# Fewer unread products in the begin, and tile loads split into two transfers

## The chip, the cores and the metric

The kernel runs on one core of one Trainium2 chip. Its time is the device time of that core in microseconds (us). The engines of a core are TensorE (PE in the profile, with its weight loads as PEld), VectorE (DVE), ScalarE (ACT), GpSimd (POOL) and SyncE (SP, which in this kernel issues all transfers between HBM and the on-chip memory SBUF). Matrix products are written to PSUM, which is read by DVE and ACT. Each engine works through its own list of instructions in order, and an instruction waits on semaphores for what it needs.

## The reference

Three stages follow each other. Attention is in chunks: 4 batches, 8 heads, 768 positions, 64 values a head. Each chunk of 32 queries sees 8 memory keys, up to 16 keys to its left, its own 32 and up to 8 to its right:

```
scores = (q_c @ k_full.T) / sqrt(64)
a = exp(scores - max(scores));  a = a / (sum(a) + 1e-9)
out[c] = a @ v_full
```

The result is a matrix of 3072 tokens by 512. Two layers follow, each with a matrix of 512 x 2048 and one of 2048 x 512, held as 64-bit floats:

```
h = x @ w1_in;  x = (h * clip(h + 3, 0, 6) / 6) @ w1_out
h = x @ w2_in;  out = max(0.01 * h, h) @ w2_out
```

## The kernel before, in words

**Tiling.** The tokens are in six blocks of 512. A weight tile `f` (16 for each of the four matrices) is 128 x 512. A weight or an activation is split into a high part, rounded to the fast 32-bit format of PE, and the low part that is left; a product is then three products (high by high, low by high, high by low), each 128x512 on PE. `hidden` (products on L998) makes one tile of `h` for one block, `output` (L1047) adds its share to four banks of the result. Later parts (`seven`, `second`; L1322 and L1490) work on pairs of blocks with seven products in the place of eight.

**Weights.** `decode` (from L386) loads a tile of 64-bit floats as pairs of 32-bit words, 4096 bytes a partition, by one transfer (`load`, L393), and builds 32-bit floats from the bits: `scaled` (L396) on ACT, then `bits` (L400), `sign` (L404) and `low` (L408) on DVE. `split_w` makes high (a cast, L341) and low (a difference, L344).

**Attention.** `unit(j, quad)` is one attention unit: four heads, 384 positions. `half_unit(j, quad, gp)` is half of one. The begin has `unit(0, 0)`, `unit(0, 1)`, `half_unit(1, 0, 0)`, `half_unit(1, 1, 0)`, then the two other half units; their results are the first blocks. A unit loads queries and keys (`load_qk`: L491, two groups of chunks in one transfer, 448 KB; in a half unit L769, two pairs of heads in one transfer) and values (`load_v`, `load_whole`); copies keys into windows (`windows`, on DVE, ACT or POOL); makes scores (L544; L811 in a half unit), the softmax on DVE and ACT (L561 to L598; L825 to L862), transposes (L602; L866), copies them out of PSUM (`take_p`), and multiplies with the values (L622; L882). `to_x` casts the result to `xh` (ACT, L341) and takes the rest as `xl` (DVE, L344).

**Unread products.** `warm(n, after, home)` (L461) puts products of the identity with itself on PE: with no `home` in a bank of their own, `n` of 512 columns; with a `home` `n` of 256 columns, in the upper half of the second bank of that buffer. Their result is read by nobody. The last argument's buffer is `ac`, in which `half_unit(1, 1, 0)` has its scores. Each product is recorded as two. A group is tied to a mark: `s` scores, `t` transposes, `v` values of a unit or half unit, and its key (its rank) is just behind the mark's. Four groups come first, and five more in a loop at L1565.

**The order.** `schedule` is a planner that runs while the program is built. It simulates the engines, with a cost for each task, takes on each engine the ready task with the smallest key, and writes the instructions in that order. Transfers are counted by their issues and bytes, with eight in flight on SP (`LANES`); a task may be said to have several issues (`issues`). It also counts PE's instructions: 447 held at the start, 256 more at each fetch (`HELD`, `FETCHED`, `FETCH`). All tasks are ranked by `key`; loads of the begin have their keys in `LOADS` and `WEIGHTS`. A change of a cost, of issues or of a task can therefore move other instructions as well.

Of the kernel before, what the change touches and what calls it, by code (L numbers as in the profile page):

```python
# [9 lines left out]
F32 = mybir.dt.float32  # L10
F32R = mybir.dt.float32r
U32 = mybir.dt.uint32
# [5 lines left out]
B, H, S, D, NMEM = 4, 8, 768, 64, 8  # L18
# [5 lines left out]
QK = 2 * G + 2 * KW  # L24
# [32 lines left out]
RATE_QK, RATE, RATE_V, COLD = 380.0, 220.0, 300.0, 1.1  # L57
# [198 lines left out]
def tile_attn_moe_moe2(ctx: ExitStack, tc: tile.TileContext, raw, w1i, w1o, w2i, w2o, out):  # L256
    nc = tc.nc
# [24 lines left out]
    def make(b, kind=None):  # L282
        if b.tag in ("hx", "y") and b.tag not in pools:

            (attention if b.tag == "hx" else begin).close()
            pools[b.tag] = (ctx.enter_context(tc.tile_pool(name=b.tag, bufs=places[b.tag], space=PSUM, side="right" if b.tag == "hx" else "left")), [128, 512], F32)
        pool, shape, dt = pools[b.tag]
        if kind is not None:
            shape, dt = kind
        b.t = pool.tile(shape, dt, tag=b.tag, name=b.tag)  # L290
        return b.t
# [35 lines left out]
    def dma(nbytes, rate=250.0):  # L327
        return nbytes / rate
# [3 lines left out]
    def add(fn, opts, key, **kw):  # L332
        t = Task(fn, opts, key, **kw)
        tasks.append(t)
        return t
# [52 lines left out]
    def decode(src, f, key, early=None, after=(), place="wm", gate=(), late=0, own=True, split=None):  # L388

        t, m = Buf("w"), Buf(place)  # L390

        def load(e):
            nc.sync.dma_start(out=make(t, ([128, 512, 2], U32)).rearrange("p w s -> p (w s)"), in_=src[f])  # L393

        def scaled(e):
            nc.scalar.mul(make(m, ([128, 512], F32)), t.t[:, :, 1].bitcast(F32), SCALED)  # L396

        def bits(e):
            mu = m.t.bitcast(U32)
            nc.vector.tensor_scalar(out=mu, in0=mu, scalar1=3, scalar2=0x7FFFFFF8, op0=ALU.logical_shift_left, op1=ALU.bitwise_and)  # L400

        def sign(e):
            mu = m.t.bitcast(U32)
            nc.vector.scalar_tensor_tensor(out=mu, in0=t.t[:, :, 1], scalar=0x80000000, in1=mu, op0=ALU.bitwise_and, op1=ALU.bitwise_or)  # L404

        def low(e):
            mu = m.t.bitcast(U32)
            nc.vector.scalar_tensor_tensor(out=mu if own else t.t[:, :, 0], in0=t.t[:, :, 0], scalar=29, in1=mu, op0=ALU.logical_shift_right, op1=ALU.bitwise_or)  # L408

        k = add(load, {"SP": dma(524288, 380.0)}, key - 30 if early is None else early, after=after, allocs=[t])  # L410
        k = add(scaled, {"ACT": act(512)}, key, after=[k, *gate], allocs=[m], uses=[t], late=late)
        k = add(bits, {"DVE": dve2(512)}, key + 0.2, after=[k], uses=[m], late=late)
        k = add(sign, {"DVE": dve(512)}, key + 0.3, after=[k], uses=[m, t], late=late)
        if split is not None:
            w = Buf("w")
            k = add(lambda e: copy(e, make(w)[:, 0, :], m.t), {"ACT": act(512), "DVE": dve2(512)}, key + 1, after=[k], allocs=[w], uses=[m])
            wbuf[split, f], wtask[split, f] = w, (k,)
        k2 = add(low, {"DVE": dve(512)}, key + 0.4, after=[k], uses=[m, t], late=late)
        return (m, k2) if own else (m, t, k, k2)
# [21 lines left out]
    xbuf, xdone, turn, sent = {}, {}, [], {}  # L441
# [23 lines left out]
    def unit(j, quad, key, tag, own=False, direct=False, loads=None):  # L465


        b, half = divmod(j, 2)
        hps, g0 = slice(2 * quad, 2 * quad + 2), 4 * half
        roomy = j in ROOMY  # L470
        e = Buf("w" if own or roomy else "a")
        qk, kw = ([Buf("w" if own or x and roomy else "a") for _ in range(2)] for x in range(2))
        v = [Buf("w" if own or roomy else "a") for _ in range(2)]
        mx, s = Buf("mx"), Buf("mx")
# [2 lines left out]
        jb, at = divmod(j * NU, N)  # L477
        first = min(NU, N - at)

        def both_groups(hp):  # L480

            a = raw[b, hp, g0, D:, :QK]
            row = a.ap[0][0]
            return bass.AP(tensor=a.tensor, offset=a.offset, ap=[[row, 128], [2 * 128 * row, 2], a.ap[1]])

        def of_raw(par, rows, cols):
            return raw[b, hps, g0 + par:g0 + 4:2, rows, cols]

        def load_qk(i):
            def fn(eng):  # L490
                nc.sync.dma_start(out=make(qk[i], ([128, 2, QK], F32)), in_=both_groups(2 * quad + i))  # L491
            return fn

        def load_v(i):
# [217 lines left out]
                sent.setdefault(c, []).append(k)  # L712

        loads = loads or (key - 50, key - 50, key - 38, key - 38)
        l1 = [add(load_qk(i), {"SP": dma(128 * 2 * QK * 4, RATE_QK)}, loads[i], after=() if own else turn, allocs=[qk[i]]) for i in range(2)]
        t = [add(windows(i), ({"DVE": 850.0} if i or quad else {"ACT": 1050.0}) if j == 0 else {"ACT": 1050.0}, key - 30, after=[l1[i]], allocs=[kw[i]], uses=[qk[i]]) for i in range(2)]
        l2 = [add(load_whole(i) if plain else load_v(i), {"SP": dma(128 * 2 * NC * 512, RATE_V if plain else RATE)}, loads[2 + i], after=() if own else t, allocs=[v[i]], issues=3 if plain else 6, loads=plain) for i in range(2)]
        if plain:
# [1 line left out]
        t = marks["s", j, quad] = add(scores, {"PE": (COLD if direct else 1.0) * 1300.0}, key - 16, ins=192, after=t, allocs=[ps], uses=[*qk, *kw])  # L720
        scored = t
        if direct and quad in SHIFT:
            t = add(greatest, {"DVE": 2100.0}, key - 15, after=[t], allocs=[mx, e], uses=[ps])
            t = add(exp_all, {"ACT": act(2 * PAIRS * W)}, key - 13, after=[t], uses=[e])
            t = add(total, {"DVE": 1250.0}, key - 12, after=[t], allocs=[s], uses=[e])
        else:
            t = add(greatest, {"DVE": 1200.0}, key - 15, after=[t], allocs=[mx], uses=[ps])
            t = add(exp(0), {"ACT": 6 * 330.0}, key - 13, after=[t], allocs=[e, s], uses=[ps, mx])
            if not own:
                turn[:] = [scored] if roomy else [t, *l2]  # L730
            t = add(exp(1), {"ACT": 6 * 330.0}, key - 13, after=[t], uses=[ps, mx, e, s])
            t = add(total, {"DVE": 350.0}, key - 12, after=[t], uses=[s])
        t = add(norm, {"DVE": 900.0} if direct else {"POOL": 1800.0, "DVE": 900.0}, key - 11, after=[t], uses=[e, s])
        t = marks["t", j, quad] = add(transpose, {"PE": (COLD if direct else 1.0) * 600.0}, key - 7, ins=12, after=[t], uses=[e, ps])
        t = add(take_p, {"ACT": act(PAIRS * 128)}, key - 5, after=[t], uses=[pt, e])
        t = marks["v", j, quad] = add(values_whole if plain else values, {"PE": (COLD if direct else 1.0) * 1600.0}, key, ins=192, after=[t, *l2], uses=[e, *v, ps])
# [12 lines left out]
    def half_unit(j, quad, gp, key, tag, loads, copies, cold):  # L749


        b, second_half = divmod(j, 2)
        g0 = 4 * second_half + 2 * gp
        qk, kw, v, e = (Buf("w") for _ in range(4))
        mx, s = Buf("mx"), Buf("mx")
# [10 lines left out]
        def load_qk(eng):  # L766
            a = raw[b, hps, g0, D:, :QK]
            there = bass.AP(tensor=a.tensor, offset=a.offset, ap=[[a.ap[1][0], 128], a.ap[0], a.ap[2]])
            nc.sync.dma_start(out=make(qk, ([128, 2, QK], F32)), in_=there)  # L769

        def load_v(eng):
            make(v, ([128, 2, NC, 2 * D], F32))
# [169 lines left out]
            if not blk:  # L942
                behind[:] = [a1]

        l1 = add(load_qk, {"SP": dma(128 * 2 * QK * 4, RATE_QK)}, loads[0], allocs=[qk])
        l2 = add(load_v, {"SP": dma(128 * 2 * NC * 512, RATE_V)}, loads[1], allocs=[v], issues=4 if whole else 8, loads=not gp)
        if whole:
            l2 = add(memory, {"POOL": 1500.0}, key - 20, after=[l2], uses=[v])
        t = add(windows, {copies: {"ACT": 1050.0, "DVE": 700.0, "POOL": 1800.0}[copies]}, key - 30, after=[l1], allocs=[kw], uses=[qk])
        t = marks["s", j, quad, gp] = add(scores, {"PE": cold * 650.0}, key - 16, ins=96, after=[t], allocs=banks, uses=[qk, kw])  # L950
        marks["b", j, quad, gp] = banks
        if gp or quad not in SHIFT_HALF:
            t = add(greatest, {"DVE": 700.0}, key - 15, after=[t], allocs=[mx], uses=banks)
            t = add(exp, {"ACT": 6 * 330.0}, key - 13, after=[t], allocs=[e, s], uses=[*banks, mx])
            t = add(total, {"DVE": 350.0}, key - 12, after=[t], uses=[s])
        else:
            t = add(greatest, {"DVE": 1250.0}, key - 15, after=[t], allocs=[mx, e], uses=banks)
            t = add(exp_all, {"ACT": act(2 * NC * W)}, key - 13, after=[t], uses=[e])
            t = add(total, {"DVE": 800.0}, key - 12, after=[t], allocs=[s], uses=[e])
        t = add(norm, {"DVE": 500.0}, key - 11, after=[t], uses=[e, s])  # L960
        t = marks["t", j, quad, gp] = add(transpose, {"PE": cold * 300.0}, key - 7, ins=6, after=[t], uses=[e, *banks])
        t = add(take_p, {"ACT": act(NC * 128)}, key - 5, after=[t], uses=[*banks, e])
# [599 lines left out]
    warm(2, marks["s", 0, 1])  # L1562
    warm(1, marks["s", 1, 0, 0])
    home = marks["b", 1, 1, 0][0]
    for m, n in ((("s", 1, 1, 0), 2), (("t", 0, 0), 3), (("t", 0, 1), 3), (("t", 1, 1, 0), 2), (("v", 1, 0, 0), 2)):  # L1565
        warm(n, marks[m], home)
    for u in range(2):
        half_unit(1, u, 1, -20.0 + 6.0 * u, "at", LOADS[4 + u], "ACT", 1.0)
# [8 lines left out]
    splits, early = [], WEIGHTS  # L1577
    for f in range(KF):
        for which, src, at in (("1i", w1i, pos_h["1", int(f >= KF // 2), f]), ("1o", w1o, pos_y["1", int(f >= KF // 2), f])):
            i = 2 * f + (which == "1o")  # L1580
# [33 lines left out]
    for kind, j, f, *n in seq2:  # L1614
        if kind == "p":
            p, i, n = j, f, n[0]
# [69 lines left out]
```

## Time and profile before

| what | before |
|---|---|
| median of 3 runs | 1044.6 us (1043.4 to 1045.1) |
| the profiled execution | 1042.63 us, span 1040.9 us |
| mean granted clock of PE | 0.997 |
| PE busy | 1030.1 us (99%) |
| DVE busy | 855.1 us (82%) |
| ACT busy | 692.6 us (67%) |
| transfers | 220.50 MB, mean 212 GB/s |

The span runs from the first to the last instruction that the profile counts. The granted clock is a share of 2.4 GHz. An engine's busy share is a mean over the whole span; a stage is read from the stretches, the timeline and the chain of waits. In the timeline, a number in brackets is how long the engine was idle ahead of the instruction, and what released it; a record "x4" is four instructions merged. Waits that a transfer's landing ends are put down to the transfer's tile.

### The profile page before, as it was taken

The page shows a single profiled execution, that of the slowest core. Times are in us where ns is not written, and L with a number is a line of the kernel's source. Part 1 is how long each engine was busy: PE and PEld are TensorE (multiplying, and loading weights), DVE is VectorE, ACT ScalarE, POOL GpSimd, SP SyncE. Part 2 cuts the span into 40 slices and gives each one's busy share as a digit, 9 for nine tenths or more (in the row PEclk, how much of TensorE's full clock was granted, in tenths as well). Part 3 has the DMA queues.
Part 4 walks back from the last instruction along what each step waited for, and adds up shares of the span by engine and source line. Part 5 has one row for each costly group of instructions (what it writes and reads, how often), then busy time and mean ns, then how long its engine had stood idle before and what let it go on. Part 6 is the DMA issues. An engine that isn't in the chain of part 4 may idle for free.

```text
span 1040.9 us, 20153 instructions
## 1 busy us (share of the span) xinstructions
PE 1030.1 (99%) x7476; PEld 849.9 (82%) x7476; DVE 855.1 (82%) x1423; ACT 692.6 (67%) x1478; POOL 22.3 (2%) x30
## 2 busy tenths in 40 slices
PE   7999999999999999999999999999999999999998
PEld 4788988888888888888888888888888888888887
DVE  6896897578999887599999898999466998566775
ACT  4896776656888554576786576775565874666753
POOL 4010000000000000000000000000000000000000
PEclk9999999999999999999999999999999999999999
DMA  9889787887897989464638894456342564522451
GB/s 266 297 241 324 258 281 238 254 293 221 286 315 232 328 280 322 157 214 135 215 129 281 268 299 151 152 170 204 128 156 81 182 200 143 179 105 99 144 182 61
DMA packets 127315, 220.50 MB, mean 212 GB/s; under 512 B 12528, under 2 KB 76016, under 8 KB 127216
## 3 DMA queue, kind: packets, MB, share of 16 engines
q1 hardware_dynamic: 127216, 219.20, 63.1%
q8 instruction: 59, 0.97, 0.4%
q14 instruction: 40, 0.33, 0.1%
HBM read 156.24 MB, written 62.91 MB: 211 GB/s over the span
## 4 chain that ended last, share of the span: by engine, by line
PE 96%; DMA 1%; DVE 1%; ACT 1%; issue 0%; SPq 0%; ACTq 0%; DVEq 0%
PE y L1322 17%; PE y L1047 15%; PE y L1490 13%; PE h L1322 11%; PE h L1490 8%; PE hx L1490 8%; PE hx L1322 8%; PE h L998 8%; PE h L1047 2%; PE at L634 2%; DMA w<-in_raw 1%; PE at L544 1%; PE at L602 1%; PE ac L461 1%; ACT w L845 0%; PE at L622 0%
## 5 line engine op out<-in xcount | busy, mean ns | idle before, releaser
L344 DVE TENSOR_TENSOR w<-w 128x512 fp32r<-128x512 f32 (+2 forms) x407 | 333.4, 858 | 28.6 <-ACT w L341 28.2
L341 ACT CAST w<-w 128x512 fp32r<-128x512 f32 (+1 forms) x296 | 226.5, 799 | 16.6 <-DMA w<-floats 7.2
L1322 PE MATMUL y<-w 128*128 128x512 f32 x516 | 124.5, 390 | 0.0
L1047 PE MATMUL y<-g,w 128*128 128x512 f32 (+1 forms) x540 | 124.4, 374 | 0.0
L1322 PEld LDWEIGHTS y<-w 128*128 128x128 f32 x516 | 96.7, 188 | 19.9
L1047 PEld LDWEIGHTS y<-g,w 128*128 128x128 f32 x540 | 94.2, 189 | 17.3
L341 ACT CAST g<-w 128x512 fp32r<-128x512 f32 x80 | 49.7, 622 | 67.6 <-PE y L1490 22.3
L1490 PE MATMUL y<-w 128*128 128x512 f32 x384 | 90.3, 389 | 0.0
L1490 PEld LDWEIGHTS y<-w 128*128 128x128 f32 x384 | 72.1, 188 | 14.9
L1296 ACT ACTIVATE w<-w 128x512 f32<-128x512 f32 x72 | 45.2, 631 | 43.0 <-DVE w L1289 21.5
L344 DVE TENSOR_TENSOR g<-w,g 128x512 fp32r<-128x512 f32 x80 | 54.8, 694 | 14.6 <-ACT g L341 14.4
L998 PE MATMUL h<-xh,w 128*128 128x512 f32 (+1 forms) x288 | 66.0, 370 | 0.0
L1490 PE MATMUL h<-w 128*128 128x512 f32 x264 | 62.1, 389 | 0.0
L1490 PE MATMUL hx<-w 128*128 128x512 f32 x252 | 59.2, 389 | 0.0
L1322 PE MATMUL h<-xl,w 128*128 128x512 f32 x240 | 58.2, 390 | 0.0
L1490 PEld LDWEIGHTS h<-w 128*128 128x128 f32 x264 | 49.6, 188 | 10.2
L998 PEld LDWEIGHTS h<-xh,w 128*128 128x128 f32 x288 | 49.7, 189 | 8.9
L1490 PEld LDWEIGHTS hx<-w 128*128 128x128 f32 x252 | 47.3, 188 | 9.8
L1322 PEld LDWEIGHTS h<-xl,w 128*128 128x128 f32 x240 | 44.9, 188 | 9.3
L1322 PE MATMUL y<-xh,w 128*128 128x512 f32 x216 | 52.0, 390 | 0.0
L1367 DVE TENSOR_TENSOR w<-y,w 128x512 f32<-128x512 f32 x35 | 24.0, 691 | 29.7 <-PE y L1322 26.9
L1322 PEld LDWEIGHTS y<-xh,w 128*128 128x128 f32 x216 | 40.5, 188 | 8.4
(243 smaller groups left out, 1836.5 us busy)
## 6 DMA issues: line engine op xcount, KB each, us to landing
w<-kept2i SPq DMA_DIRECT2D x42, 512.0 KB
w<-kept2o SPq DMA_DIRECT2D x42, 512.0 KB
w<-kept1i SPq DMA_DIRECT2D x28, 512.0 KB
a<-in_raw SPq DMA_DIRECT2D x20, 448.0 KB
w<-in_w1i SPq DMA_DIRECT2D x16, 512.0 KB
w<-in_w1o SPq DMA_DIRECT2D x16, 512.0 KB
w<-in_w2i SPq DMA_DIRECT2D x16, 512.0 KB
w<-in_w2o SPq DMA_DIRECT2D x16, 512.0 KB
```

The source lines that it names most:

```text
L341: nc.scalar.copy(out, in_) if e == "ACT" else engine(e).tensor_copy(out=out, in_=in_)
L344: engine(e).tensor_tensor(out=out, in0=a, in1=b, op=ALU.subtract)
L461: nc.tensor.matmul(x, ident, ident.unsqueeze(1).to_broadcast([128, c, 128]), start=True, stop=True, skip_group_check=True)
L544: nc.tensor.matmul(ps.t[h * CHUNK:(h + 1) * CHUNK, par, i * W:(i + 1) * W], qk[h // 2].t[r, gp, (h % 2) * G + c * CHUNK:(h % 2) * G + (c + ...
L602: nc.tensor.transpose(pt.t[:, i // NC, (i % NC) * 128:(i % NC + 1) * 128], pview()[:, i * 128:(i + 1) * 128], ident)
L634: nc.tensor.matmul(pv.t[(h % 2) * D:(h % 2 + 1) * D, par, (h // 2) * 2 * G + i * CHUNK:(h // 2) * 2 * G + (i + 1) * CHUNK], v[h // 2].t[r, ...
L998: nc.tensor.matmul(h.t[:, o:o + n], w.t[:, 1 if p == 1 else 0, k * 128:(k + 1) * 128], x[:, k, c0:c0 + n], start=(p == 0 and k == 0 and o ...
L1047: nc.tensor.matmul(bank(banks[d])[:, c0:c0 + n], w.t[:, 1 if p == 1 else 0, d * 128:(d + 1) * 128], g.t[:, 1 if p == 2 else 0, at:at + n], ...
L1296: return add(lambda e: nc.scalar.activation(out=at(), in_=at(), func=AF.Prelu, alpha=0.01), {"ACT": act(N)}, key, after=[after], uses=uses)
L1322: nc.tensor.matmul(bank(to), wt(l, o)[:, kt * 128:(kt + 1) * 128].bitcast(F32R), operand(p, name, 1 if q == 2 else 0, kt).bitcast(F32R), s ...
L1367: done[2] = add(lambda e: nc.vector.tensor_tensor(out=half_of(x, 0), in0=bank(bb), in1=ut.t[:, 0], op=ALU.add), low, key, after=[k, done[1 ...
L1490: nc.tensor.matmul(bank(to[d]), wt(1 if q == 1 else 0, o)[:, d * 128:(d + 1) * 128].bitcast(F32R), g.t[:, 1 if q == 2 else 0], start=(fres ...
```

## The change

Of the five groups in the loop two stay, those after the transposes of `unit(0, 0)` and `unit(0, 1)`. A weight tile is loaded by two transfers of 256 values (2048 bytes a partition) each; queries and keys of a unit by one transfer for each group of chunks, and those of a half unit by one for each pair of heads. The planner is told of two issues for each of these tasks. The tasks that read a tile are as before.

```diff
         def load(e):
-            nc.sync.dma_start(out=make(t, ([128, 512, 2], U32)).rearrange("p w s -> p (w s)"), in_=src[f])
+            make(t, ([128, 512, 2], U32))
+            for x in (0, 256):
+                nc.sync.dma_start(out=t.t[:, x:x + 256].rearrange("p w s -> p (w s)"), in_=src[f, :, 2 * x:2 * x + 512])
...
-        k = add(load, {"SP": dma(524288, 380.0)}, key - 30 if early is None else early, after=after, allocs=[t])
+        k = add(load, {"SP": dma(524288, 380.0)}, key - 30 if early is None else early, after=after, allocs=[t], issues=2)
...
-        def both_groups(hp):
+        def both_groups(hp, gp):
 
-            a = raw[b, hp, g0, D:, :QK]
-            row = a.ap[0][0]
-            return bass.AP(tensor=a.tensor, offset=a.offset, ap=[[row, 128], [2 * 128 * row, 2], a.ap[1]])
+            a = raw[b, hp, g0 + 2 * gp, D:, :QK]
+            return bass.AP(tensor=a.tensor, offset=a.offset, ap=[[a.ap[0][0], 128], a.ap[1]])
...
-                nc.sync.dma_start(out=make(qk[i], ([128, 2, QK], F32)), in_=both_groups(2 * quad + i))
+                make(qk[i], ([128, 2, QK], F32))
+                for gp in range(2):
+                    nc.sync.dma_start(out=qk[i].t[:, gp], in_=both_groups(2 * quad + i, gp))
...
-        l1 = [add(load_qk(i), {"SP": dma(128 * 2 * QK * 4, RATE_QK)}, loads[i], after=() if own else turn, allocs=[qk[i]]) for i in range(2)]
+        l1 = [add(load_qk(i), {"SP": dma(128 * 2 * QK * 4, RATE_QK)}, loads[i], after=() if own else turn, allocs=[qk[i]], issues=2) for i in range(2)]
...
-            nc.sync.dma_start(out=make(qk, ([128, 2, QK], F32)), in_=there)
+            make(qk, ([128, 2, QK], F32))
+            for i in range(2):
+                nc.sync.dma_start(out=qk.t[:, i], in_=bass.AP(tensor=a.tensor, offset=there[:, i].offset, ap=[there.ap[0], there.ap[2]]))
...
-        l1 = add(load_qk, {"SP": dma(128 * 2 * QK * 4, RATE_QK)}, loads[0], allocs=[qk])
+        l1 = add(load_qk, {"SP": dma(128 * 2 * QK * 4, RATE_QK)}, loads[0], allocs=[qk], issues=2)
...
-    for m, n in ((("s", 1, 1, 0), 2), (("t", 0, 0), 3), (("t", 0, 1), 3), (("t", 1, 1, 0), 2), (("v", 1, 0, 0), 2)):
+    for m, n in ((("t", 0, 0), 3), (("t", 0, 1), 3), ):
         warm(n, marks[m], home)
```

## Rows read from the trace of the kernel before

**Rows 1.** the page's first part: engines' busy us, share of the span, instructions.

```profile
PE 1030.1 (99%) x7476; PEld 849.9 (82%) x7476; DVE 855.1 (82%) x1423; ACT 692.6 (67%) x1478; POOL 22.3 (2%) x30
```

**Rows 2.** busy us by stretch (us from start): engines, granted clock, DMA share, GB/s.

```profile
440.00:490.00 50.00, 50.00 (x222) 41.45 (x221) 50.00 (x79) 35.19 (x54) 0.00 (x0) 1.00 0.51 168
...
sum 1001.00, PE 995.75 PEld 826.48 DVE 827.92 ACT 670.87 POOL 11.31; mean PE 49.79 PEld 41.32 DVE 41.40 ACT 33.54 POOL 0.57
```

**Rows 3.** waits of PE from 45 us on: total us, times, longest.

```profile
PE at L602 <- DVE w L598: 0.9, 1, 0.9
```

**Rows 4.** chain of waits, 0 to 60 us: start us, us, engine, tile, line.

```profile
20.54 1.89 ACT w L845 x12
...
30.96 0.29 ACT w L341
...
44.34 1.14 PE at L894 x47
45.48 2.94 PE y L1047 x12
```

**Rows 5.** timeline of PE: start us, us, line, tiles, [idle before <-releaser].

```profile
14.12 0.45 PE L811 MATMUL h<-w 64*32 64x64 f32 x29 [0.65 <-issue]
...
17.50 0.84 PE L602 MATMUL at<-ident,w 128*128 128x128 f32 x6 [0.25 <-DVE w L598]
18.94 1.56 PE L461 MATMUL ac<-ident 128*128 128x256 f32 x6 [0.59 <-DVE mx L825]
22.47 1.13 PE L461 MATMUL ac<-ident 128*128 128x256 f32 x4 [1.97 <-ACT w L845]
23.53 2.92 PE L622 MATMUL at<-w 64*64 64x32 f32 x96
26.38 1.54 PE L602 MATMUL ab<-ident,w 128*128 128x128 f32 x6
27.72 2.77 PE L461 MATMUL ac<-ident 128*128 128x256 f32 x6
...
31.13 1.78 PE L622 MATMUL ab<-w 64*64 64x32 f32 x96
32.84 1.13 PE L461 MATMUL ac<-ident 128*128 128x256 f32 x4
33.90 0.98 PE L882 MATMUL h<-w 64*64 64x32 f32 x48
34.81 1.13 PE L461 MATMUL ac<-ident 128*128 128x256 f32 x4
...
37.44 2.11 PE L998 MATMUL h<-xh,w 128*128 128x512 f32 x8
```

**Rows 6.** busy us by stretch again, single microseconds of the begin.

```profile
23.00:24.00 1.00, 1.00 (x23) 0.66 (x22) 1.00 (x2) 0.54 (x1) 1.00 (x1) 0.83 0.48 102
...
29.00:30.00 1.00, 1.00 (x4) 0.81 (x3) 1.00 (x3) 0.32 (x1) 0.00 (x0) 0.50 1.00 391
30.00:31.00 1.00, 1.00 (x8) 0.76 (x6) 0.53 (x1) 0.04 (x1) 0.00 (x0) 0.76 1.03 335
```

**Rows 7.** waits of DVE, 20 to 46 us.

```profile
DVE wm L400 <- ACT wm L396: 1.9, 1, 1.9
DVE xl L344 <- ACT xh L341: 1.4, 1, 1.4
```

**Rows 8.** DMA issues, L393 and L491: ns min/median/max, first and last us.

```profile
L393 SPq DMA_DIRECT2D w<-in_w1i x16: 362/444/1242, 11.1 to 144.4; - x16
...
L491 SPq DMA_DIRECT2D w<-in_raw x8: 395/460/680, 0.7 to 57.9; - x8
```

**Rows 9.** timeline of SP's issues, 0 to 62 us.

```profile
22.20 0.59 SPq L393 DMA_DIRECT2D w<-in_w1i  x1
...
26.43 0.27 SPq L787 DMA_DIRECT2D w<-in_raw  x1
```

**Rows 10.** timeline of ACT, 20 to 46 us.

```profile
31.71 0.68 ACT L396 ACTIVATE wm<-w 128x512 f32<-128x512 f32 x1
```

## The prediction

> **What bounds the kernel now.** I read the engine totals first. TensorE (PE) is busy 99% of the span, VectorE (DVE) 82% [rows 1]. An average over 1041 us hides stages, so the next view is busy time in stretches: from 40 us to the end PE is busy 995.75 of 1001 us, and in 440 to 490 us DVE has not one idle moment while PE has none either [rows 2]. The list of waits for PE from 45 us on has a single entry, 0.9 us [rows 3]. So behind the begin nothing can be won by moving waits; there only a new wait can appear. The 45 us before it are another matter, and the chain of waits shows what they are made of: small pieces that hop between PE, ScalarE (ACT) and DVE. It runs through ACT at 20.54, then on PE from the group at 22.47, goes to ACT at 30.96, stays on ACT and DVE, and returns to PE at 44.34, just ahead of the first `output` products [rows 4].
>
> PE's own list of the begin shows what the removed groups are [rows 5]. The line L461 is `warm`: products of the identity with itself, which nobody reads. The five late groups stand at 18.94 (after the first transposes, six records for n=3), 22.47 (the group of `s 1 1 0`, four records for n=2), 27.72 (`t 0 1`), 32.84 (`t 1 1 0`) and 34.81 (`v 1 0 0`). The reader is to see the idle time in the brackets: the group at 22.47 waited 1.97 us for ACT, whose exponentials read another part of the same bank; and `values` at 23.53 stood behind it on PE's queue, although its own operand had been copied from PSUM before (the transposes at 17.50 end near 18.3).
>
> The same list shows the clock. The 96 products of `values` take 2.92 us at 23.53 and 1.78 us at 31.13, the transposes 1.54 us at 26.38 and 0.84 at 17.50, the six unread products 2.77 us at 27.72 and 1.56 at 18.94 [rows 5]. The granted clock falls from 1.00 to 0.50 (1.2 of 2.4 GHz) within the microsecond from 23, and comes back between 30 and 31 [rows 6]. What PE did before it fell: idle from 20.50 to 22.47.
>
> **The change, part by part.**
>
> *The group of `s 1 1 0` goes.* PE stood from 20.50 (the end of the group at 18.94) to 23.53: 1.97 us of waiting and 1.06 us of products, 3.03 us. `values` can then start at 20.50. Next on PE's queue are the transposes of the second unit, which wait for nothing there now either [rows 5]. So nothing is late next here.
>
> *The groups of `t 1 1 0` and `v 1 0 0` go.* From 32.84 to the next instruction it is 1.06 us, and the other has the same four records: 2.12 us of PE [rows 5]. In that stretch the chain is on ACT and DVE [rows 4], so by themselves they are worth little.
>
> *The clock.* Without the 1.97 us gap I expect no fall at 23.5. The three groups above then cost 1.14 + 0.70 + 1.21 = 3.05 us less. Bounds: 0 (it falls there all the same) and 3.05; I take 3.05, since the one long gap ahead of the fall goes.
>
> PE alone thus gives 3.03 + 2.12 + 3.05 = 8.2 us. That is not the gain, because the chain leaves PE at 30.96. From there DVE works nearly without a pause, and what an earlier PE can save is DVE's idle time in 20 to 46 us: 1.9 us before L400 and 1.4 us before `xl` [rows 7]. The second of these was a wait for the cast of `values`' result, the first for ACT, which itself had waited for transposes on the late PE. Replaying DVE's order with both gone, each step from `xl` of the second unit on comes 3.3 us earlier, and so does the first `output` group (45.48 to 42.2). The term has 3.3 us as its value, 8.2 as its upper bound (the planner lets ACT and DVE do first what PE waits for, and puts weights off) and 0 as its lower (see the rivals).
>
> *Two transfers instead of one.* `decode` issues 64 loads, `load_qk` 28 in the units and 4 in the half units [rows 8], so 96 more issues at 0.44 to 0.46 us (the medians), about 43 us of SP over the whole kernel. The bytes stay, and so does the order in which they are asked for, as far as the planner keeps it. Nobody reads a half: the `windows` copies and the `scaled` activation take the whole tile, so no consumer starts earlier. The cost is in the queue. The planner counts eight transfers in flight (LANES), and SP stands until one of them has landed. With halves the eight hold fewer bytes. The load that can be late is that of the second `w1i` tile: issued at 22.20, landed by 26.43, when SP's next issue that waited for it went out [rows 9]. ACT takes it at 31.71 now [rows 10], at 28.4 after a shift of 3.3, a margin of 2.0 us. Ahead of it stand five more issues (two key tiles, two weight tiles, its own second half), 5 x 0.44 = 2.2 us if SP never waited anyway, nothing if it did. The cost is between 0 and 0.2 us by that; I take 0.3 so as to leave some room for the loads behind it. Of the later weight loads none is waited for by PE now [rows 3]: what they are early by covers the second issue, and without that cover each would cost its 0.44 us. The wire is no slower in one respect that the trace shows: tiles of 512 KB move at 391 GB/s with the engines full [rows 6].
>
> The Trainium skill (DMA: Bandwidth & Descriptors, "Rules for kernel authors") speaks against the halves: it wants a megabyte and more per transfer for full bandwidth. Taken at its word the loads get slower and the sum falls short of 3.0, by an amount that neither the page nor a row gives for halves. No row of this trace has a half tile by itself, so the sum goes by the issue times.
>
> Sum: -3.3 + 0.3 = -3.0 us. The profiled execution took 1042.63 us (span 1040.9, so 1.7 us lie around it), which gives 1039.6. The median of the three runs shown is 1044.6, 2.0 us above the profiled one; the same difference gives 1041.6.
>
> **The rivals.**
>
> *The clock falls at another place.* With two groups gone at 32.84 and 34.81, PE has a new gap: the last `values` of the half units would be done near 29 to 30 us, and the first hidden products (L998, at 37.44 now [rows 5]) wait for ACT's cast of that result, 33.6 at the latest. For: a gap of 1.97 us preceded the fall at 23.5, and this one can be 3 us or more. Against: if ACT does that cast first, the gap is about a microsecond. At half clock, hidden and output products double, on PE's path; the stretch at 23.5 cost 3.05 us, so 3.3 - 3.05 leaves 0.3: 1044.3 us. The Trainium skill (TensorE: Matmul & The Clock Gate, "Why this matters for your kernels") advises against idle gaps between bursts because the clock drops back; by that rule this rival holds, and the row of the fall after an idle PE agrees with it.
>
> *PE's instructions come late.* At 14.12 PE stood 0.65 us for "issue" and no semaphore [rows 5]. Up to there the program has 221 products, 442 instructions with their weight loads, near the 447 that the planner takes as held (HELD), with 256 more per fetch. A faster PE meets the next borders (959 and 1215 instructions) at about 26 and 29 us instead of 32 and 36.4. If each fetch takes as long as from the first border to the next one used (5 us in the planner's FETCH, an estimate there), the last `values` group waits to 32 to 34 us. DVE is the bound up to 34, so the loss is up to 1.5 us: 1043.1.
>
> *PE gets all of it.* 8.2 us: 1036.4. For: the keys rank the casts of attention before the decoding of weights. Against: DVE stays full behind it.
>
> *Slower: new waits behind the begin.* `issues=2` and the missing groups change the planner's times, and with them the order of DVE, ACT and SP all through. Where DVE has no idle time (440 to 490 us [rows 2]) a DVE operation that is put later stops PE. Price: the one wait there is costs 0.9 us [rows 3]; six such waits 5.4, less 3.0, is +2.4: 1047.0. It decides from four waits on, and it tells from no change from six. For: there is no slack on either engine there. Against: over the whole stretch from 40 us DVE has 17% to spare (827.92 of 1001 us busy [rows 2]).
>
> **How the numbers follow.** A measurement of this kernel tells 0.2%, 2.1 us, from no change. The forecast (gain 2.1 to 4.5 us) 0.44; the clock 0.22; the instructions 0.08; all of PE's gain 0.08; slower 0.18. Faster by over 2.1 us is 0.44 + 0.08 = 0.52; slower takes 0.18 and 0.02 of the clock's case, where the gap is long: 0.20; the rest, 0.28, lies within. The range runs from 1037.0, which takes in most of the case of all of PE's gain, to 1047.3, a little above the priced slow case; about 0.06 is left out below and 0.12 above. The likeliest case's own range is 1040.1 to 1042.5.
>
> **What would show it.** The first group of 12 `output` products should start near 42.5 instead of 45.48. `values` of the first unit should start near 20.5 and take about 1.8 us; if it takes 2.9 the clock term is wrong. DVE's waits before L400 and `xl` in 20 to 46 us should be under 0.5 us in all. The granted clock should read 1.00 in every microsecond from 16 to 46 us; 0.50 in 29 to 42 us is the first rival. An "issue" of over 1 us on PE near 26 to 33 us is the second. The list of PE's waits from 45 us on should stay under 1.5 us; over 3 us there, with the first output group early, is the slow case. I am wrong altogether if the first output group is not earlier, or if it is 6 us earlier.

## The result, and the profile after

| | before | after |
|---|---|---|
| median (range) | 1044.42 us (1043.4 to 1045.1) | 1055.28 us (1053.69 to 1056.12), 4 runs |
| ratio, 95% interval | | 1.0100 (1.0085 to 1.0115) |
| the profiled execution, span | 1042.63, 1040.9 us | 1053.69, 1051.5 us |
| PE busy | 1030.1 us | 1027.8 us |

The change makes the kernel 10.4 us slower (1.0% of 1044), where 3.0 us faster was forecast. PE has less to do and idles more: the span less PE's busy time is 10.8 us before and 23.7 after. Three stretches say where. The columns are as in [rows 2]: length, then busy us of PE, PEld, DVE, ACT and POOL, the granted clock, the DMA share and GB/s. First before, then after:

```profile
0.00:45.00 45.00, 38.71 (x738) 26.66 (x739) 32.15 (x86) 26.77 (x99) 10.96 (x23) 0.92 0.86 263
45.00:250.00 205.00, 204.05 (x2556) 171.61 (x2549) 166.14 (x319) 145.91 (x453) 6.28 (x4) 1.00 0.83 273
250.00:1040.90 790.90, 787.35 (x4199) 651.61 (x4197) 656.82 (x1020) 519.96 (x929) 5.03 (x3) 1.00 0.57 193
```

```profile
0.00:45.00 45.00, 32.44 (x695) 22.48 (x696) 31.82 (x86) 25.82 (x98) 10.58 (x23) 0.89 0.85 236
45.00:250.00 205.00, 197.64 (x2530) 164.98 (x2529) 157.81 (x302) 141.55 (x440) 4.67 (x3) 0.99 0.82 262
250.00:1051.50 801.50, 797.71 (x4243) 659.13 (x4241) 665.13 (x1038) 526.79 (x943) 1.47 (x1) 1.00 0.59 195
```

In the begin PE idles 12.6 us instead of 6.3; from 45 to 250 us 7.4 instead of 0.95; behind that 3.8 and 3.6. The saved work of the begin went into idle time there, and 6.4 us of new idle time came in the stretch behind it.

The begin on PE, which answers [rows 5]:

```profile
19.04 1.56 PE L463 MATMUL ac<-ident 128*128 128x256 f32 x6 [0.59 <-DVE mx L830]
20.53 0.83 PE L625 MATMUL at<-w 64*64 64x32 f32 x36
21.59 1.24 PE L625 MATMUL at<-w 64*64 64x32 f32 x60 [0.23 <-issue]
...
25.52 1.78 PE L625 MATMUL ab<-w 64*64 64x32 f32 x96
...
27.90 0.69 PE L887 MATMUL ac<-w 64*64 64x32 f32 x31
30.60 0.80 PE L887 MATMUL ac<-w 64*64 64x32 f32 x17 [2.01 <-issue]
36.44 1.46 PE L816 MATMUL at<-w 64*32 64x64 f32 x48 [5.04 <-DMA w<-in_raw]
37.82 3.10 PE L1003 MATMUL h<-xh,w 128*128 128x512 f32 x8
...
44.64 1.18 PE L1052 MATMUL y<-g,w 128*128 128x512 f32 x4
...
46.60 1.66 PE L1052 MATMUL y<-g,w 128*128 128x512 f32 x6
```

To 28.6 us it went as forecast on PE: `values` at 20.53 (23.53 before) and at full clock, and those of the second unit at 25.52 (31.13). Then PE stands 2.01 us for "issue" and 5.04 us for a transfer, and the first hidden products start at 37.82 (37.44). Of the first twelve `output` products four stand at 44.64 and eight from 46.60; before, all twelve stood together from 45.48 [rows 4]. Nothing of the 5.6 us is left.

The clock, which answers [rows 6]. It does not fall at 23 us now; it falls when PE stands at 29.8 and comes back at 40:

```profile
23.00:24.00 1.00, 1.00 (x9) 0.95 (x8) 0.97 (x3) 1.00 (x6) 0.00 (x0) 1.00 0.65 174
29.00:30.00 1.00, 0.00 (x0) 0.00 (x0) 1.00 (x3) 1.00 (x7) 0.00 (x0) 0.88 0.86 199
30.00:31.00 1.00, 0.40 (x13) 0.41 (x14) 1.00 (x3) 0.74 (x4) 0.00 (x0) 0.50 0.87 307
...
39.00:40.00 1.00, 1.00 (x4) 0.81 (x3) 1.00 (x4) 0.94 (x7) 0.00 (x0) 0.50 0.79 295
```

PE's waits from 45 us on, which answer [rows 3] (one entry of 0.9 us there). They sum to 7.4 us; behind the longest, at 118 us, the clock is at half once more for 3.4 us:

```profile
PE y L1052 <- ACT g L341: 2.3, 1, 2.3
PE at L547 <- issue: 1.8, 3, 1.2
PE at L605 <- POOL w L601: 1.3, 1, 1.3
PE at L871 <- DVE w L867: 0.8, 1, 0.8
PE at L605 <- DVE w L601: 0.5, 1, 0.5
PE at L637 <- ACT w L341: 0.4, 1, 0.4
PE y L1327 <- ACT xh L341: 0.3, 1, 0.3
```

DVE's waits in 20 to 46 us, which answer [rows 7]: the one before L400 shrank, the one before `xl` doubled.

```profile
DVE xl L344 <- ACT xh L341: 2.8, 1, 2.8
DVE wm L402 <- ACT wm L398: 0.9, 1, 0.9
```

Why `xl` waits is in ACT's own list: it stood 4.02 us for a key tile, and the cast `xh<-ac`, whose input PE had ready at 31.4, was queued behind the copies of those keys.

```profile
31.14 0.61 ACT L341 CAST w<-ys 128x512 fp32r<-128x512 f32 x1
35.78 1.11 ACT L341 COPY w<-w 128x336 f32<-128x336 f32 x4 [4.02 <-DMA w<-in_raw]
36.79 0.65 ACT L341 CAST xh<-ac 128x128 fp32r<-128x128 f32 x4
```

Before, ACT made these copies at 35.42 and waited for nothing:

```profile
35.42 1.14 ACT L341 COPY w<-w 128x336 f32<-128x336 f32 x4
```

SP's list, which answers [rows 9], has the second `w1i` tile at 23.59 instead of 22.20, a delay of 1.4 us where 0 to 2.2 were forecast, and the keys of this half unit at 28.06 instead of 24.26. First before, then after:

```profile
24.26 0.68 SPq L769 DMA_DIRECT2D w<-in_raw  x1
```

```profile
23.59 1.56 SPq L395 DMA_DIRECT2D w<-in_w1i  x2
...
28.06 1.72 SPq L774 DMA_DIRECT2D w<-in_raw  x2
```

### The profile page after: what moved, and what is told of

Read it like the earlier page. It is cut to its first block, busy times and chain, and to the rows that moved or that the text cites. A ratio compares the mean times of both kernels' runs of the same rounds, so it can differ in the third digit from the quotient of the medians.

```text
span 1051.5 us, 20275 instructions
## 1 busy us (share of the span) xinstructions
PE 1027.8 (98%) x7464; PEld 846.6 (81%) x7464; DVE 854.8 (81%) x1424; ACT 694.2 (66%) x1480; POOL 16.7 (2%) x27
## 4 chain that ended last, share of the span: by engine, by line
PE 86%; DMA 3%; DVE 2%; ACT 1%; SPq 1%; issue 1%; ACTq 0%
PE y L1327 16%; PE y L1495 12%; PE y L1052 12%; PE h L1327 11%; PE h L1495 8%; PE hx L1327 8%; PE hx L1495 8%; PE h L1003 5%; PE h L1052 2%; PE at L637 1%; DMA w<-in_w1o 1%; PE at L547 1%; PE at L605 1%; DMA half<-ys 1%; DMA w<-kept1i 1%
## 5 line engine op out<-in xcount | busy, mean ns | idle before, releaser
L344 DVE TENSOR_TENSOR w<-w 128x512 fp32r<-128x512 f32 (+2 forms) x407 | 331.9, 851 | 30.2 <-ACT w L341 29.9
```

Of the source, the lines that this page charges most:

```text
L344: engine(e).tensor_tensor(out=out, in0=a, in1=b, op=ALU.subtract)
```

## The experiments

Theory at the start: with the groups gone PE runs into the next border of its instructions and the clock falls elsewhere, so the begin gains nothing; the halves cost SP time, which makes loads late; the planner's other order adds waits. Times are medians; the before of the same chip lay between 1043.5 and 1044.6.

### One part alone

**e1_groups**: two groups, loads whole.

```diff
-    for m, n in ((("s", 1, 1, 0), 2), (("t", 0, 0), 3), (("t", 0, 1), 3), (("t", 1, 1, 0), 2), (("v", 1, 0, 0), 2)):
+    for m, n in ((("t", 0, 0), 3), (("t", 0, 1), 3), ):
```

> Two late groups of unread products instead of five, loads whole as before. Theory Q (the halves cost: each load takes two of the eight places in flight on SP and a second issue, so what is behind it lands later): the keys of the third half unit are issued near 24.5 us and land before ACT is free for them, no wait of PE over 1 us for a transfer in 0 to 60 us; 1041 to 1046 us. Rival O (the planner's other order behind the begin costs, whatever caused it): about 630 of PE's instructions, 340 of DVE's stand elsewhere here too, so 1049 to 1056. Rival W (without the groups PE's clock falls and its instructions come late): half clock between 28 and 42 us, 1047 to 1050.

1049.29 us, ratio 1.0049 (1.0031 to 1.0068): slower by itself. That the keys would land in time with whole loads was not so: ACT stood 4.22 us for them.

**e2_loads**: after, with the five groups of before.

> Loads as two transfers, and the planner told so; all five groups kept. Theory Q: nearly the whole loss of the changed kernel, 1051 to 1056 us, with waits for transfers in 60 to 180 us. Rival O: the same, since the order is another here too. Rival W: 1044 to 1046, the loads cost nothing.

1054.38 us, 1.0090 (1.0056 to 1.0124).

**e3_split_untold**: as e2_loads, but the planner is not told. The order of every engine is that of before; 96 transfers stand in SP's list in addition. The cut is against e2_loads:

```diff
-... early, after=after, allocs=[t], issues=2)
+... early, after=after, allocs=[t])
```

> Loads as two transfers, the planner told of one, five groups: each engine's order is that of the kernel before, save the 96 second transfers on SP. Theory Q: 1050 to 1056 us, slower by as much as the loads alone with the planner told. Rival O: 1043.5 to 1046, as the order is that of before. Rival W: the same as O here.

1052.46 us, 1.0076 (1.0050 to 1.0102).

**e4_whole_told**: loads whole, but the planner is told of two issues, so that it writes the order of e2_loads.

```diff
-        l1 = add(load_qk, {"SP": dma(128 * 2 * QK * 4, RATE_QK)}, loads[0], allocs=[qk])
+        l1 = add(load_qk, {"SP": dma(128 * 2 * QK * 4, RATE_QK)}, loads[0], allocs=[qk], issues=2)
...
```

> Loads whole as before, but the planner told of two issues, five groups: the order is that of the loads split and told (no engine but SP differs from it), the transfers are those of before. Theory Q: 1042 to 1047 us. Rival O: 1050 to 1056. Rival W: 1044 to 1046.

1043.66 us, 0.9996 (0.9976 to 1.0015). So the order that `issues=2` alone brings costs nothing that can be seen, and the transfers themselves cost 7.9 us (5.2 to 10.7).

### The groups without the planner's other order

**e8_absent**: the planner counts all five groups, but three write no products; loads whole. **e11_one_absent**: only the group of `s 1 1 0` is left out, in the same way.

```diff
+        gone = after in left_out
...
-            for _ in range(n):
+            for _ in range(0 if gone else n):
```

> Loads whole; the three groups (after s 1 1 0, t 1 1 0, v 1 0 0) are left out of the program, but the planner still counts them: each engine's order is that of the kernel before, PE without six unread products. With the planner told (another order) it measured 1049.3. Theory G (PE, ahead of its feeders, stands at the border of a block of instructions and then at half clock, so the begin gains nothing; the rest of that loss is new waits that come from the other order): first output products within 1 us of 45.5, 1043 to 1046 us. Rival C (the clock and the instructions themselves cost the 4.9 us): 1047 to 1050. The prediction's own step (3.3 us earlier) would be 1040 to 1042.

> Loads whole; only the group after s 1 1 0, for which values stood in line, is left out of the program; the planner still counts it, so every other instruction stands as before. Theory G: PE comes early to the border of a block of instructions (after 600 to 602 products) and stands there for 2 to 4 us, so the first output products come within 1 us of 45.5, and the time is 1042.5 to 1045.5; with the two other groups in place the half clock is shorter than 10.2 us. The prediction's step would have them at 42 to 43 and the time at 1040 to 1042.

e8_absent 1044.66 us, 1.0008 (0.9997 to 1.0018); e11_one_absent 1044.8 us, 1.0002 (0.9990 to 1.0013). Neither gains, although `values` starts earlier. PE's timeline of e8_absent:

```profile
27.23 0.69 PE L884 MATMUL ac<-w 64*64 64x32 f32 x30
31.71 0.80 PE L884 MATMUL ac<-w 64*64 64x32 f32 x18 [3.79 <-issue]
34.64 1.46 PE L813 MATMUL at<-w 64*32 64x64 f32 x48 [2.13 <-ACT w L341]
36.03 3.78 PE L1000 MATMUL h<-xh,w 128*128 128x512 f32 x8
```

Two things end there at nearly one time. PE's instructions come 3.79 us late (the profile says "issue", that is, PE waits for nothing that it shows; that the instructions have not arrived is read from the fixed count of products, in the last section). And ACT, with whole loads too, stands 3.46 us for the keys of the third half unit, asked for at 24.56 (24.26 in before):

```profile
29.88 0.65 ACT L341 CAST xh<-h 128x128 fp32r<-128x128 f32 x4
33.98 1.11 ACT L341 COPY w<-w 128x336 f32<-128x336 f32 x4 [3.46 <-DMA w<-in_raw]
```

The clock is at half from 30.0 to 40.2: eight hidden products take 3.78 us instead of 2.11 [rows 5].

As e1_groups and e8_absent differ only in what the planner knows, the 4.1 us between them (1.0049 and 1.0008, intervals apart) are the planner's other order: e1_groups has PE waits of 5.2 us behind 45 us, e8_absent 2.1.

### Which of the two ends the begin

The keys of the third half unit are asked for earlier. **e15_keys_first**: three weight tiles earlier, groups out as in e8_absent. **e17_keys_one_ahead**: one tile earlier (-133.5), so that SP's order alone changes. **e16_before_keys_first**: before, with the keys three tiles earlier.

```diff
-LOADS = (..., (-120, -118), (-116, -114))
+LOADS = (..., (-135.5, -118), (-116, -114))
```

> The three late groups are left out of the program as before, loads whole, but the keys of the third half unit are asked for three weight tiles earlier (SP's order; the planner also takes ACT's copies of them ahead of five casts). If the landing of these keys is what keeps the begin from gaining (ACT stood 3.46 us for them with the groups out), that wait falls below 1 us, the first output products come 2 to 4 us before the 45.93 they had, and the time is 1 to 3 us below before. If PE's late instructions are the bound (3.79 us at a fixed count), the wait for the keys goes but PE stands as long, and the first output products stay at 45 to 46 us.

> The three late groups out, loads whole, and the keys of the third half unit one weight tile earlier: SP's order alone changes, by one place. If their landing is the bound, ACT's wait of 3.46 us shortens by the time of one tile, some 1.3 us, and the first output products come about as much earlier than 45.93. If PE's late instructions are the bound, they stay.

> Before, all five groups in, with the keys of the third half unit three weight tiles earlier. ACT does not wait for these keys in before, so the begin should not change by itself: within 1 us of before. A gain of more would mean that the keys' place helps without the groups going.

1043.87, 1044.84 and 1043.99 us; ratios 1.0004 (0.9991 to 1.0017), 1.0004 (0.9990 to 1.0018) and 1.0004 (0.9994 to 1.0015). In e15_keys_first ACT has its key copies at 29.88 instead of 33.98 (it still stands 1.85 us for them, not under 1), and PE no longer waits for them. The stand for instructions stays, and so does the half clock behind it. PE's timeline of e15_keys_first:

```profile
33.30 0.80 PE L884 MATMUL ac<-w 64*64 64x32 f32 x18 [3.79 <-issue]
34.02 0.97 PE L813 MATMUL at<-w 64*32 64x64 f32 x48
34.92 3.78 PE L1000 MATMUL h<-xh,w 128*128 128x512 f32 x8
...
45.13 3.03 PE L1049 MATMUL y<-g,w 128*128 128x512 f32 x12
```

The first `output` products come 0.8 us before those of e8_absent (45.93), and 0.3 before those of before (45.41 in this view), not 2 to 4. This execution has the clock at half from 15.8 to 22.7 us too, so PE starts `values` 1.7 us later than in e8_absent (21.48 and 19.79), and its profile alone understates what the keys gave. e17_keys_one_ahead has no such early fall: ACT's wait shrinks by 1.2 us to 2.28, the stand for instructions is 4.37 us, and the first `output` products come at 45.18, 0.75 us earlier. So the late keys hold the begin, and right behind them the late instructions with the half clock hold it nearly as long; the times, from 11 and 12 runs, show no gain either. Taking the instructions' stand away as well was not tried. No version here beats before by what can be measured.

The gap ahead of the clock's fall at 23 us does not decide the clock by itself. e16_before_keys_first has all five groups and the same gap, and its `values` run at full clock:

```profile
21.80 1.13 PE L461 MATMUL ac<-ident 128*128 128x256 f32 x4 [1.98 <-ACT w L845]
22.86 1.78 PE L622 MATMUL at<-w 64*64 64x32 f32 x96
```

e2_loads, e4_whole_told and e5_weights_only do the same with gaps of 1.97 and 1.98 us; in e3_split_untold, e6_keys_only, e7_pool, e9_pause, e10_long_pause and e13_by_rows the clock falls there as in before. Where it does not fall, little is won: PE, now early, stands 1.29 us for instructions at 34.38 in e16_before_keys_first, the clock falls behind that, and the first `output` products come at 45.01. In e4_whole_told, in another order, the granted clock is 1.00 in every microsecond to 46 us and they come at 43.66, yet its span is 1040.5 us against 1040.9 in before.

### What in the halves costs

**e5_weights_only** (64 more transfers) and **e6_keys_only** (32 more): one of the two sorts of tiles split, planner not told.

> Only the weight tiles as two transfers, queries and keys whole, five groups, the planner told of one issue: each engine's order is that of the kernel before, save 64 second transfers on SP. All halves in that order measured 1052.5 (1047 to 1054). Theory Q (SP is never idle in the first 45 us, so each further issue delays all that stands behind it): the weights are two thirds of the added issues, and the begin's keys come first, so 1047 to 1051. Rival K (it is the key loads, on whose landing PE's first products wait): 1043.5 to 1046.

> Only queries and keys as two transfers (32 further issues), weights whole, five groups, order of before. The weights alone measured 1048.6, both 1052.5. Theory Q, by count of issues: a third of the whole loss, 1045.5 to 1048. If what counts is that the keys themselves land late: 1047.5 to 1050. If the keys' halves cost nothing: 1043 to 1045.

1048.56 us, 1.0042 (1.0024 to 1.0059), and 1048.75 us, 1.0031 (1.0015 to 1.0048): 4.4 and 3.2 us, together 7.6, near the 7.9 of both. Each sort costs, so it is not one late tile.

**e9_pause** and **e10_long_pause**: whole loads, and two or eight drains of SP behind each. A drain is an instruction that waits for SP's own earlier ones; it holds SP and moves nothing.

```diff
             nc.sync.dma_start(out=make(t, ([128, 512, 2], U32)).rearrange("p w s -> p (w s)"), in_=src[f])
+            for _ in range(8):
+                nc.sync.drain()
```

> Loads whole, five groups, order of before; behind each weight and key load SP runs two instructions that wait for its own earlier instructions and move nothing (96 loads). They cost SP time, but take no place in flight and move no bytes. Theory Q with issue time as its part: later issues by what the two take on SP (to be read in the trace), 1045 to 1052 if it is 0.2 us and more for a load. If the places in flight are what costs: 1043 to 1045.5.

> As the kernel with pauses on SP behind each whole load, but with eight instructions instead of two, about 0.45 us for a load by the shorter one's trace (four key loads took 2.41 us with two, 1.97 without): as long as the second issue of a split load, with no place in flight taken and no bytes moved. Theory Q, issue time alone: as slow as the loads split with the order kept, 1048 to 1054. If places in flight are the larger part: 1044 to 1047.

1045.71 us, 1.0013 (0.9997 to 1.0029), and 1048.44 us, 1.0037 (1.0024 to 1.0051). SP's first four key loads took 1.97 us in before, 2.41 with two drains, 3.34 with eight and 3.71 as halves; so eight drains are about a second issue ((3.34 - 1.97) / 3 = 0.46 us between two loads), and SP's time alone costs 3.9 us of the 7.9.

**e14_tiny**: whole loads, and behind each a transfer of 16 rows of 8 bytes that nobody reads.

```diff
             nc.sync.dma_start(out=make(t, ([128, 512, 2], U32)).rearrange("p w s -> p (w s)"), in_=src[f])
+            nc.sync.dma_start(out=spare[:, next(tiny)], in_=src[f, :16, :2])
```

> Leaves the loads whole and puts a transfer of 16 rows of 8 bytes into an unread place behind each of the 96 loads; order of all engines as before. If SP's issues and the places among the transfers in flight are what the halves cost, it takes about as much as the halves did, +6 to +9 us (1050 to 1053). If the halves' smaller packets or their doubled row count matter as well, it takes only what the issue time alone costs, about +4 us (1048 to 1049), as eight pauses of SP behind each load did. If neither, within 1 us of before.

1050.72 us, 1.0068 (1.0053 to 1.0082): 7.1 us, close to the halves, at packets and bytes of the loads as before. So it is the number of transfers, not their size, as far as these intervals tell. A tiny one holds SP as long as a 448 KB one; SP's timeline of e14_tiny:

```profile
0.74 0.44 SPq L494 DMA_DIRECT2D w<-in_raw  x1
1.23 0.45 SPq L495 DMA_DIRECT2D spare<-in_raw  x1
```

**e13_by_rows**: weight tiles in two transfers of 64 whole partitions.

```diff
+            for x in (0, 64):
+                nc.sync.dma_start(out=t.t[x:x + 64].rearrange("p w s -> p (w s)"), in_=src[f, x:x + 64])
```

> Weight tiles only in two transfers, each of 64 partitions whole (packets of 4096 bytes) instead of 256 columns of all 128; 64 more issues, order as before. The same split by columns cost 4.2 to 4.6 us. If the number of transfers is the cause, the same again: 1048.5 to 1049.5. If the smaller packets are, it falls to 2 us or less: below 1046.5.

1069.39 us, 1.0239 (1.0214 to 1.0264): neither case. It split by another cost, which hides the one it was for: such halves move at about half the rate. From 25 to 30 us, first before and then e13_by_rows:

```profile
25.00:30.00 5.00, 5.00 (x64) 4.46 (x61) 3.58 (x8) 2.30 (x6) 1.36 (x2) 0.50 1.01 401
```

```profile
25.00:30.00 5.00, 5.00 (x46) 4.29 (x43) 3.10 (x8) 2.31 (x6) 2.85 (x4) 0.50 0.90 212
```

The transfer engines are nearly as full (0.90 and 1.01), at 212 instead of 401 GB/s. The Trainium skill (DMA: Bandwidth & Descriptors, "Rules for kernel authors") advises one transfer over all 128 partitions in the place of two over disjoint halves; this run agrees, at a cost of 25.0 us (22.4 to 27.6).

**e7_pool**: halves, the second ones issued by GpSimd, planner not told.

```diff
-                nc.sync.dma_start(out=t.t[:, x:x + 256]...
+                (nc.gpsimd if x else nc.sync).dma_start(out=t.t[:, x:x + 256]...
```

> All loads as two transfers, but the second one is issued by GpSimd in the same place of the order; five groups, planner told of one. SP has as many issues as before, and the halves are as small as in the changed kernel. Theory Q (SP's time and its places in flight): 1043 to 1047. Rival B (smaller rows and more descriptors slow the wire itself): as slow as with both halves on SP, 1050 to 1054. GpSimd's own copies of the begin may come later behind its issues, which could cost 1 to 2 us in either case.

1055.3 us, 1.0107 (1.0086 to 1.0129), and inconclusive: GpSimd's halves ran ahead of SP's (a half of `w1i` was issued at 4.79 us, ahead of keys at 9.02), and its own copies came late (13.23 instead of 9.92).

**e12_both_untold**: the instructions of after in the order of before, that is halves and three groups out, and the planner told of neither.

> The changed kernel's instructions in the order of the kernel before: loads as two transfers, three groups left out, the planner told of neither. The changed kernel measured 1055.3. If its loss is the halves (8.0 with the order kept) and the groups add nothing with the order kept (0.8): 1051 to 1055. If the planner's order carried a good part of it: 1047 to 1050.

1050.45 us, 1.0056 (1.0038 to 1.0075): 5.9 us. From there to after (1.0100) it is 4.6 us, the planner's other order again, as between e8_absent and e1_groups.

How late loads reach PE shows in ACT's waits for transfers between 45 and 250 us. In before these are all:

```profile
ACT ys L396 <- DMA half<-ys: 1.1, 1, 1.1
ACT w L341 <- DMA w<-in_raw: 0.8, 1, 0.8
ACT ys L396 <- DMA floats<-ys: 0.6, 1, 0.6
```

and in e3_split_untold, in the same order of instructions (this execution took 1047.08 us, the shortest of the five):

```profile
ACT w L341 <- DMA a<-in_raw: 2.9, 2, 1.8
ACT w L341 <- DMA w<-in_raw: 2.7, 2, 2.0
ACT ys L398 <- DMA half<-ys: 2.7, 1, 2.7
ACT wm L398 <- DMA w<-in_w1i: 1.1, 2, 0.8
ACT ys L398 <- DMA floats<-ys: 1.0, 1, 1.0
```

2.5 us have become 10.4, with stores among them (`half`, `floats`), which stand in SP's list behind the loads. PE's waits behind 45 us sum to 0.9 us in before, 3.6 in e3_split_untold and 5.3 in e14_tiny. These sums show the path and not the price: ACT's are 13.5 us in e14_tiny and 15.9 in e10_long_pause, which costs less.

## Why the prediction was wrong

**The halves, +0.3: the step that failed most.** The prediction worked out 43 us of extra issues and put them beside the path: "what they are early by covers the second issue". Measured with the order kept, +7.9 us. The stated bound was "each would cost its 0.44 us" without cover, 42 us: cover took most of that, but not all, and the sum left 0.3 us for everything. A margin was worked out for one tile, 2.0 us, and for that tile it held (ACT took it at 28.27; 28.4 was forecast). What mattered is SP as an engine that issues everything: summed over its timeline it issues 29.9 us and waits 13.4 us for landings in the first 45 us of before; in after 35.8 and 7.9. Issues and these waits leave it less than 2 us. Most of the further issue time came off the waits for landings, and still SP came later to what is behind in its list, by 1.4 us at the second `w1i` tile and by 3.8 at the keys behind it. The wire is not what cost the time: the share of the loads' queue is 63.1% of the span in before, 63.9% in e3_split_untold and 62.4% in e12_both_untold at the same bytes, and e14_tiny costs nearly as much without any halves. So the rule of the Trainium skill weighed there (DMA: Bandwidth & Descriptors, "Rules for kernel authors") had the right sign, but no run shows a lower bandwidth of these halves as the cause.

**The begin, -3.3: the cap was put on the wrong engine.** The pieces on PE came as forecast: the group's 3.03 us, the full clock at 23 us, `values` at 20.53. "What an earlier PE can save is DVE's idle time" was not: e8_absent, which has just this part, takes 0.8 us more than before (-0.3 to +1.9), where 3.3 less were forecast. Late next were the keys of the third half unit. The replay gave a margin for the second `w1i` tile, and none for these keys, which were asked for behind four weight tiles, at 24.26, while the transfer engines were full. At the same place PE's instructions come 3.79 us late, and the clock is at half for 10 us. These are the first two rivals, both real: the stand at "issue" over 1 us near 28 to 32 us, and 0.50 in 30 to 40 us, were named as signs. Each was priced alone, at 2.7 and 1.5 us less gain than forecast (the first without the 0.3 for the halves); with the keys they took all of it. The reason given for the clock's 3.05 us, that the long gap ahead of the fall goes, is not borne out: with the same gap of 1.97 or 1.98 us the clock stayed at 1.00 in four executions (e16_before_keys_first above). The Trainium skill's advice against idle gaps (TensorE: Matmul & The Clock Gate, "Why this matters for your kernels") agrees with after in part: the clock fell at 29.8 us, in a stand of PE, but whether it falls behind the 1.97 us gap these runs do not tell.

**The planner's other order: the rival on the slower side was real, and its net price too low.** It was priced at 5.4 us for six new waits of 0.9, less the forecast's gain of 3.0. The waits behind 45 us are seven entries in after, 6.5 us more than in before, and two pairs of runs give 4.1 and 4.6 us for the order. Its price was right in size; the gain that was taken off it did not exist. The place was not: only 0.3 us of these waits lie behind 250 us, none in 440 to 490 us, where DVE was full and the rival had put them. Nor did the order that `issues=2` brings cost anything that can be seen (e4_whole_told, -0.4 us; e2_loads and e3_split_untold, 1.0090 and 1.0076, with overlapping intervals). What costs is the order that the planner writes for the missing groups (e1_groups against e8_absent).

**The sum as measured**: halves and groups in the order of before 5.9 us (4.0 to 7.8; alone 7.9 and 0.8), the order 4.6 us, together 10.4. The range ended at 1047.3, as no case had the halves cost more than 0.3 us.

**What stays open.** Of the halves' 7.9 us SP's time alone explains 3.9 (2.5 to 5.3), the tiny transfers 7.1 (5.5 to 8.6). What a transfer costs beyond the time of its issue, some 3 us here over 96, was not settled: places among those in flight and the waits for their landing are candidates, and no run separates them. The profiles of e10_long_pause and e14_tiny cannot: the two executions took 1050.3 and 1050.28 us, with 5.3 us of PE's waits behind 45 us in each. Nor was a run made without PE's stand for instructions.

## What to carry to other kernels

Count a queue's issues as busy time of an engine before splitting a transfer: where that engine has no free time, 96 issues of 0.44 us cost 7 to 8 us even though no product waits for any one of the tiles now. A removed wait is worth what the next late thing leaves, and every operand of the next instructions on every in-order engine has to be replayed, the loads asked for last above all. Where a planner writes the order, change a cost or a task with the order held fixed first; here one other order cost 4 to 5 us and another nothing. A clock that falls in one profile may stay up in the next at the same gap, so a gain that rests on it wants more than one trace.

## What was not expected of the hardware

- PE stood for its instructions at one count of products in kernels of different timing: 3.70, 3.79, 3.79 and 4.37 us after the 30th of 48 products at one place (e1_groups, e8_absent, e15_keys_first, e17_keys_one_ahead). With one group out it was 2.70 us after the 23rd, two other groups' products standing ahead of it. Counted from the start it is always after 600 to 602 products: in 13 of the 19 kernels, for 0.81 to 4.37 us, also with all five groups in (after the 20th of the 48). In before and five others, all with the clock at half ahead of this place, there is no such stand.
- At one gap of 1.97 to 2.02 us on PE, at one place of the program, the clock fell in some executions and not in others.
- A transfer of 128 bytes holds SP for 0.45 us, one of 448 KB for 0.43.
- Two transfers of 64 partitions in the place of one of 128 moved 212 GB/s with the transfer engines 90% busy, against 401.
